# Two decode layers on one core: output weights of two key heads loaded as four adjacent rows a partition

## The chip, the cores and the metric

The kernel runs on one core of a Trainium2 chip. The metric is the device time of one execution in microseconds, as the median of several runs; lower is better. A profile is one more execution, recorded by the hardware profiler; times within it count from the first instruction of that execution.

## What is computed

Two identical layers for four sequences with one new token each. A layer is attention over a cached context, with 32 query heads in 8 key heads (4 query heads share a key head), followed by a feed-forward block. Both layers use the same caches and weights, all in bfloat16.

```python
def _A_ref(x, k_cache, v_cache, wq, wo):
    q = (x @ wq)  # as [4, 32, 1, 128]
    ...
    scores = jnp.einsum("bhqd,bhkd->bhqk", q, k) * (Dh ** -0.5)
    p = _softmax(scores, axis=-1)
    o = jnp.einsum("bhqk,bhkd->bhqd", p, v)
    return (lambda x, *d: x.transpose(*d))(o, 0, 2, 1, 3).reshape(B, Sq, Hq * Dh) @ wo

def _B_ref(x, w_gate, w_up, w_down):
    return (_gelu(x @ w_gate) * (x @ w_up)) @ w_down

x = A_x
x = x + _A_ref(_layernorm(x, axis=-1), A_k_cache, A_v_cache, A_wq, A_wo)
x = x + _B_ref(_layernorm(x, axis=-1), B_w_gate, B_w_up, B_w_down)
...
```

The last two lines are done a second time. Shapes: x is 4 x 512, each cache 4 sequences x 8 key heads x 4096 positions x 128, `wq` 512 x 4096, `wo` 4096 x 512, the feed-forward weights 512 x 1792 and 1792 x 512. One sequence's keys or values of one key head are 1 MB, so the caches are 64 MB in all.

## The kernel before, in words

**Order of the work.** `attend_first` does sequence 0 of layer 1. Then a loop runs over the sequences b = 0 to 3: the feed-forward block of layer 1 for b (`dense_first` for 0, `dense` for the others), and then a stage that mixes layer 2 of sequence b with layer 1 of sequence b + 1 (`attend(b + 1)`). Where the prediction speaks of sequence 1, 2 or 3, it means layer 1 of that sequence, the second half of `attend(1)`, `attend(2)` and `attend(3)`. After the last block come `attend_last`, layer 2 of sequence 3 (the last stage), and `dense_last`, the feed-forward of layer 2 for all four sequences at once. Layer 2 reuses a few value tiles that layer 1 left in place; most of the cache is read twice.

**Tiles and buffers.** A cache tile is half of one key head's context, 128 partitions with 16 positions of 128 numbers, 4 KB a partition and 512 KB in all. Eight value tiles have slots (`VRing`, L682), keys have sixteen. Every load is issued on SyncE's queue (SP), in program order. A value load is issued as soon as the step that last used its slot has ended, so the ring of slots paces the loads. All instructions of an engine run in the order that the program gives.

**Value steps.** `Values.step` (L828) multiplies one value tile with the softmax's probabilities. For a streamed head the result is in rows (`stream_v`, L786, matmuls of L791); DVE turns it (`turn_v`, L799) and sums and scales it (`sum_v`, L801, with L806 and L807) into `OT_bf` or, in layer 2, `OT2_bf`: attention outputs with the 128 numbers of a head on the partitions and the heads along the free axis. Unstreamed heads use L859 and are scaled by L680; the last head of a sequence is one of them. Scaling is done when a head, or a pair of heads, has both its tiles; `hold=True` puts it off until `flush`. Results lie in PSUM, in two banks in turn; in `attend` the streamed heads of the second group use the banks `ps_sc`, `ps_sm` and `ps_sc`, and the last head `ps_sm` again.

**Output weights.** `wo_sb` holds, for each of the 32 query heads, 128 rows of 512, row d on partition d: 1 KB a partition and head. `load_rest` (L158) loads it in four pieces of eight heads, at the end of `attend_first`, with the feed-forward weights behind it on the queue. `RowProj.heads` (L401) multiplies a head's output with its weights into 512-wide rows (matmul of L405, four heads in four column groups at a time); `split` (L409) brings the row sums to bfloat16 in two parts, with a ScalarE copy (L412) and a DVE operation (L413); `onto` adds them to the column-wise result `y`. `OutProj.heads` (L385, matmuls of `mac`, L275) does the remaining heads directly into `y`. So the final order of a sequence is: row sums of most heads, split, the last pair of heads directly, the split added, the rest of that pair.

**Fillers.** `busy(n, ...)` (L479, matmuls of L482) issues n matmuls whose result nobody reads.

**Head order.** The two groups of four key heads swap from sequence to sequence. Sequences 0 and 2 take heads 0 to 3 first, sequences 1 and 3 take heads 4 to 7 first. In `attend`, `heads` lists the pairs of key heads in the order of their value steps: row sums of `heads[0]`, `heads[1]` and `heads[2]` are placed between value steps (L1230 to L1240), `heads[3]` goes through `OutProj`. In `attend_last` (L1252) the pair of key heads 2 and 3 comes first, then 0 and 1, then 4 and 5; head 7 is the last.

**The last stage's tables.** ScalarE needs a function table for gelu; L1291 loads it ahead of the value steps of the last group.

Of the kernel before, what the change touches and what calls it, by code (L numbers as in the profile page):

```python
# [30 lines left out]
WD_PARTS = (0, 6, 10, 12, 13, 14)  # L31
ROWS_A = 8
UP_ROWS = 8


@with_exitstack
def kernel(
# [111 lines left out]
    def cache_tile(cache, b, kvh, t):  # L149
        if whole(b, kvh):  # L150
            return cache[b, kvh].rearrange("(p t c) d -> t p c d", t=NT, p=P)[t]
        return cache[b, kvh].rearrange("(t p c) d -> t p c d", t=NT, p=P)[t]

    def load_wq(g):
        n = HG * Dh
        dq.dma_start(out=wq_sb[g][:], in_=wq_dram[:, :, g * n:(g + 1) * n])

    def load_rest():  # L158
        n = Hq // 4
        for i in range(4):  # L160
            dq.dma_start(out=wo_sb[:, i * n:(i + 1) * n], in_=wo_dram[:, i * n:(i + 1) * n])  # L161
        dq.dma_start(out=wg_sb[:], in_=B_w_gate.rearrange("(k p) n -> p k n", p=P))
        dq.dma_start(out=wu_sb[:], in_=B_w_up.rearrange("(k p) n -> p k n", p=P))
        wd_dram = B_w_down.rearrange("(k p e) n -> p k e n", p=P, e=2)
        wd_pairs = wd_sb.rearrange("p (k e) n -> p k e n", e=2)
        for lo, hi in zip(WD_PARTS, WD_PARTS[1:]):
            if hi - lo > 1:
                own = slice(lo // 2, hi // 2)
                dq.dma_start(out=wd_pairs[:, own], in_=wd_dram[:, own])
            else:  # L170
                dq.dma_start(out=wd_sb[:, lo], in_=wd_dram[:, lo // 2, lo % 2])
# [201 lines left out]
    def nothing(t):  # L373
        nc.scalar.copy(out=t, in_=qb[:, 0:1].broadcast_to([P, t.shape[1]]))
# [207 lines left out]
    def scores(sc, g, t, runs=together):  # L582
        for run in runs:
            scores_of(sc, g, [(s, t) for s in run])
# [224 lines left out]

    class Values:  # L810
        def __init__(self, layer, b, tiles, prob, dst, keeps=(), streamed=(), paired=(), sums=None, park=(),
                     last_bank=None, off_ot=False, last_width=WEIGHT):
            self.streamed, self.sums, self.park = streamed, sums or {}, park
            self.paired, self.last_bank, self.off_ot = paired, last_bank, off_ot
            self.last_width = last_width
            self.layer, self.b, self.tiles, self.n = layer, b, list(tiles), 0
            self.prob, self.dst, self.keeps = prob, dst, keeps
            self.seen, self.ot, self.late = {}, None, []
# [65 lines left out]
        def unit(self, kvh):  # L884
            pair = [2 * (kvh // 2), 2 * (kvh // 2) + 1]
            alone = kvh in self.streamed and kvh not in self.paired
            return [kvh] if self.tiles[-1][0] in pair or alone else pair

        def scale(self, ot, unit, rden):
            n, s = len(unit), unit[0] % GH  # L890
            if unit[0] in self.streamed:
                turn_v(ot, n)
                return sum_v(ot, self.dst(unit[0], n), rden[:, s:s + n], n)
            scaled(self.dst(unit[0], n), ot[:, s % 2:s % 2 + n, :rep], rden[:, s:s + n])
# [64 lines left out]
    def attend_first():  # L959
# [5 lines left out]
        last = one(b)[-1][0]  # L965
        vals = Values(1, b, one(b), prob1, dst1(b), keeps=kept,
                      streamed=[h for h in range(Hkv) if h != last],
                      paired=[h for h in range(Hkv) if h // 2 != last // 2])
        ring.extend(1, b, one(b))
        load_wq(gx)  # L970
        keys.load_heads(GH)
# [40 lines left out]
        vals.step(3)  # L1012
        scores(sc1, gy, 1, last_alone)
        vals.step(3, hold=True)
        p0 = soft(sc1)
        vals.flush()
        soft_turn(p0)
# [117 lines left out]
    def attend(b, qy, before, norm, early=None):  # L1135
# [11 lines left out]
        vals1 = Values(1, b, one(b), prob1, dst1(b), keeps=kept1,  # L1147
                       streamed=[gy * GH + s for s in range(GH - 1)], park=apart1,
                       sums={4: (ps_sc, "sc"), 5: (ps_sm, "sm"), 6: (ps_sc, "sc")},
                       last_bank=lambda: ps_sm.tile([P, 2, WEIGHT], FP32, name="ot", tag="sm"))  # L1150

        sc2 = [new_scores(early=True)]
        if early:
# [59 lines left out]
        turn(4)  # L1213
        vals1.step(3)
        scores(sc1, gy, 1, last_alone)
        p0 = soft(sc1)
        vals1.step(3)
        x = swap_tile()
# [11 lines left out]
        vals1.step(2)  # L1230
        rows.heads(heads[0], hp)
        vals1.step(2)
        rows.heads(heads[1], hp)
        vals1.step(1)
        proj = OutProj(o1(b), 1)
        spare = proj.bank[:, KD * WEIGHT:]
        rows.heads(heads[2], rep)
        busy(3, spare)
        vals1.step(1)
        rows.heads(heads[2] + rep, rep)  # L1240
        rows.split()
        busy(5, spare)
        vals1.step(1)
        proj.heads(heads[3], rep)
        vals1.step(1)
        assert vals1.left() == 0
# [5 lines left out]
    def attend_last(q_bf, norm, before, late):  # L1252
        b = B - 1
        gx, gy = second_groups[b]
        prob2 = {}
        kept2, own2, other2, apart2 = two(b)
        tiles = kept2 + own2 + apart2 + other2
        vals = Values(2, b, tiles, prob2, dst2(b),
                      streamed=[h for h in range(Hkv) if h != tiles[-1][0]],
                      paired=[h for h in range(Hkv) if h // 2 != tiles[-1][0] // 2],  # L1260
                      last_width=WIDE)
        sc2 = [new_scores(early=True)]
        scores(sc2[0], gx, 0)
        ring.pump_tile(late[0], k_tile(gx * GH + 2, 0))
        ring.pump_halves(late[1], k_tile(gx * GH + 3, 0))
        scores(sc2[0], gx, 1)
        q_spread_apart(q_sums(q_bf[:]))
        p0 = soft(sc2[0], norm)
        for _ in range(2):
            before.fill()  # L1270
        before.turn()
        sc2.append(new_scores(early=True))
        scores(sc2[1], gy, 0)
        scores(sc2[1], gy, 1)
        soft_turn(p0)
        before.sum()
        pe0, den0 = soft_swap(p0), soft_den(p0)
        p1 = soft(sc2[1], norm, lasting=True)
        prob2[gx] = (pe0, soft_recip(den0))
        rows = RowProj(o2)  # L1280
        vals.step(8, hold=True)
        soft_turn(p1)
        vals.flush()
        pe1, den1 = soft_swap(p1), soft_den(p1)
        prob2[gy] = (pe1, soft_recip(den1))
        heads = pairs(tiles)
        homes = [(ps_x, "x", ROWS_A), (ps_h, "h", KF - ROWS_A)]
        full = [pool.tile([P, n * WIDE], FP32, name="gr", tag=tag) for pool, tag, n in homes]
        for part in full:
            nothing(part[:])  # L1290
        nc.scalar.preload_act_table_set("gelu_apprx_tanh_and_others")  # L1291
        vals.step(4)
        rows.heads(heads[0], hp)
        rows.heads(heads[1], hp)
        vals.step(2)
        rows.heads(heads[2], hp)
        rows.split()
        vals.step()
        proj = OutProj(o2, B, WIDE)
        proj.heads(heads[3], rep)  # L1300
        vals.step()
        rows.onto(proj)
        proj.n = Hq - rep
        proj.heads(heads[3] + rep, rep)
        part = banks.tile([P, UP_ROWS * WIDE], "ur")
        nothing(part[:])
        spare = ps_sc.tile([P, 512], FP32, name="spare", tag="sc")
        busy(1, spare[:])
        squares = wq_sb[1][:, 3].bitcast(FP32)[:, :B * (KD + 1)].rearrange("p (b k) -> p b k", b=B)
        nc.vector.memset(squares[:, :, KD], D * LN_EPS / P)  # L1310
        assert vals.left() == 0 and ring.at == len(ring.seq)
        return proj.y, full + [part], squares
# [260 lines left out]
```

## Time and profile before

| | |
|---|---|
| median of 3 runs | 268.15 us (266.75 to 268.27) |
| profiled execution, its own time | 268.99 us |
| its span, first to last instruction | 267.2 us |
| mean granted TensorE clock | 0.866 |
| TensorE matmul busy | 195.1 us (73%) |
| VectorE busy | 182.2 us (68%) |
| ScalarE busy | 66.0 us (25%) |
| moved by DMA | 103.05 MB, mean 386 GB/s |
| four loads of `wo_sb` | 1024 KB each, 12.0 us from issue to landing |

How to read it: the page cuts the span into 40 equal slices (6.68 us each) and gives, per engine, the busy share in tenths, the granted clock of TensorE (PEclk) and what the DMA engines moved. A row of the timeline has start, duration, engine, line of the kernel, operation, output and inputs, shape, count and, in brackets, how long the engine had been idle before it and what ended that wait; several equal instructions in a row are merged, so a duration of "x16" spans all sixteen. A matmul's end includes its drain, and the next may start before it. The chain that ended last is followed backwards from the last instruction: each piece was released by the one above it.

### The profile page before, as it was taken

The page shows a single profiled execution, that of the slowest core. Times are in us where ns is not written, and L with a number is a line of the kernel's source. Part 1 is how long each engine was busy: PE and PEld are TensorE (multiplying, and loading weights), DVE is VectorE, ACT ScalarE, POOL GpSimd, SP SyncE. Part 2 cuts the span into 40 slices and gives each one's busy share as a digit, 9 for nine tenths or more (in the row PEclk, how much of TensorE's full clock was granted, in tenths as well). Part 3 has the DMA queues.
Part 4 walks back from the last instruction along what each step waited for, and adds up shares of the span by engine and source line. Part 5 has one row for each costly group of instructions (what it writes and reads, how often), then busy time and mean ns, then how long its engine had stood idle before and what let it go on. Part 6 is the DMA issues. An engine that isn't in the chain of part 4 may idle for free.

```text
span 267.2 us, 8596 instructions
## 1 busy us (share of the span) xinstructions
PE 195.1 (73%) x3767; PEld 114.8 (43%) x3775; DVE 182.2 (68%) x448; ACT 66.0 (25%) x136; POOL 3.9 (1%) x10
## 2 busy tenths in 40 slices
PE   1396246544689796989678968787788687888884
PEld 1333123322255453557436245464363354553563
DVE  3385955451335899884776998746769996568773
ACT  1001001100222422032323520304136103044642
POOL 2000000000001000000000000000000000000001
PEclk9998555655597959799999985899999979999999
DMA  7999999999994999999999999999999999999940
GB/s 244 432 416 421 423 429 417 408 385 406 413 412 177 394 416 417 420 417 400 390 414 416 416 419 421 416 415 375 403 418 418 421 415 418 420 405 405 413 160 3
DMA packets 30732, 103.05 MB, mean 386 GB/s; under 512 B 2788, under 2 KB 7144, under 8 KB 29672
## 3 DMA queue, kind: packets, MB, share of 16 engines
q1 hardware_dynamic: 30672, 102.51, 95.7%
q8 instruction: 29, 0.48, 0.6%
q14 instruction: 7, 0.06, 0.1%
q10 hardware_dynamic: 24, 0.01, 0.0%
HBM read 102.50 MB, written 0.00 MB: 384 GB/s over the span
## 4 chain that ended last, share of the span: by engine, by line
DMA 51%; PE 21%; DVE 16%; SPq 6%; ACT 3%; issue 3%; DVEq 0%
DMA v_t<-in_A_v_cache_dram 25%; DMA kp<-in_A_k_cache_dram 8%; DMA kw<-in_A_k_cache_dram 8%; PE sc L592 6%; DMA wu_sb<-in_B_w_up_dram 5%; DMA kw<-in_A_v_cache_dram 4%; SPq L161 4%; DVE kp L537 3%; PE ot L859 3%; DVE kw L537 3%; PE y L275 3%; PE so L791 2%; PE q L309 1%; DVE q L315 1%; DVE qb L360 1%
## 5 line engine op out<-in xcount | busy, mean ns | idle before, releaser
L592 PE MATMUL sc<-kw,qb 128*32 128x512 bf16 x244 | 39.6, 446 | 5.2 <-DVE kw L537 2.2
L592 PE MATMUL sc<-kp,qb 128*32 128x512 bf16 x268 | 40.1, 450 | 1.0 <-DVE kp L537 0.2
L592 PEld LDWEIGHTS <-qb 128*32 128x32 bf16 x512 | 23.1, 104 | 39.6 <-issue 21.4
L537 DVE STREAM_TRANSPOSE kw<-kw 128x1024 f32<-128x1024 f32 x32 | 38.0, 1215 | 0.7 <-DMA kw<-in_A_k_cache_dram 0.6
L537 DVE STREAM_TRANSPOSE kp<-kp 128x1024 f32<-128x1024 f32 x32 | 36.7, 1199 | 0.0
L859 PE MATMUL ot<-pe,v_t 128*128 128x32 bf16 (+1 forms) x896 | 30.0, 184 | 5.6 <-DMA v_t<-in_A_v_cache_dram 2.8
L859 PEld LDWEIGHTS <-v_t 128*128 128x128 bf16 x896 | 27.7, 100 | 13.7 <-issue 7.4
L614 ACT ACTIVATE pe<-sc,nl 128x512 bf16<-128x512 f32 x8 | 5.5, 687 | 85.9 <-DVE pe L611 67.6
L791 PE MATMUL so<-v_t,pe 128*32 128x256 bf16 x304 | 15.0, 319 | 13.6 <-DMA v_t<-in_A_v_cache_dram 11.6
L799 DVE STREAM_TRANSPOSE so<-so 128x512 f32<-128x512 f32 (+1 forms) x23 | 13.8, 599 | 11.1 <-PE so L791 11.1
L791 PEld LDWEIGHTS <-pe 128*32 128x32 bf16 x320 | 9.1, 105 | 19.4 <-issue 12.5
L602 DVE TENSOR_REDUCE pe<-sc 128x1 f32<-128x512 f32 x12 | 8.3, 691 | 9.2 <-PE sc L592 9.1
L405 PE MATMUL yr<-wo_sb,OT_bf 128*2 128x512 bf16 (+1 forms) x120 | 10.7, 425 | 4.9 <-DMA wo_sb<-in_A_wo_dram 4.9
L647 PE MATMUL x<-pe,ident_bf 128*32 128x128 bf16 x192 | 5.4, 233 | 11.8 <-DVE pe L622 11.8
L647 PEld LDWEIGHTS <-ident_bf 128*32 128x32 bf16 x256 | 5.3, 100 | 16.1 <-issue 14.1
L791 PE MATMUL so<-v_t,pl 128*32 128x256 bf16 x192 | 9.4, 275 | 3.3 <-DMA v_t<-in_A_v_cache_dram 3.3
L650 ACT CAST pe<-x 128x512 bf16<-128x512 f32 x12 | 7.0, 586 | 17.4 <-PE x L647 17.4
L275 PE MATMUL q<-xb,wq_sb 128*128 128x5 bf16 (+1 forms) x192 | 5.7, 173 | 6.5 <-DMA wq_sb<-in_A_wq_dram 6.5
L353 PE MATMUL qe<-q_bf,ident_bf 128*32 128x16 bf16 (+1 forms) x272 | 5.7, 176 | 5.6 <-DVE q_bf L335 2.9
L622 DVE STREAM_TRANSPOSE pe<-pe 128x512 bf16<-128x512 bf16 x12 | 8.4, 696 | 1.1 <-ACT pe L614 1.1
L275 PEld LDWEIGHTS <-wo_sb 128*128 128x128 bf16 x160 | 7.6, 101 | 3.3 <-DMA wo_sb<-in_A_wo_dram 2.6
L482 PEld LDWEIGHTS <-ident_bf 128*128 128x128 bf16 x63 | 5.2, 99 | 8.7 <-issue 4.3
(172 smaller groups left out, 255.2 us busy)
## 6 DMA issues: line engine op xcount, KB each, us to landing
v_t<-in_A_v_cache_dram SPq DMA_DIRECT2D x89, 512.0 KB, 8.5
kp<-in_A_k_cache_dram SPq DMA_DIRECT2D x32, 512.0 KB, 9.9
kw<-in_A_k_cache_dram SPq DMA_DIRECT2D x24, 512.0 KB, 9.6
wq_sb<-in_A_wq_dram SPq DMA_DIRECT2D x2, 2048.0 KB, 7.7
kw<-in_A_k_cache_dram SPq DMA_DIRECT2D x4, 1024.0 KB, 11.6
v_t<-in_A_v_cache_dram SPq DMA_DIRECT2D x4, 1024.0 KB, 14.2
wo_sb<-in_A_wo_dram SPq DMA_DIRECT2D x4, 1024.0 KB, 12.0
wq_sb<-in_A_v_cache_dram SPq DMA_DIRECT2D x3, 1024.0 KB, 11.8
```

Source lines behind the costliest of these rows:

```text
L161: dq.dma_start(out=wo_sb[:, i * n:(i + 1) * n], in_=wo_dram[:, i * n:(i + 1) * n])
L275: nc.tensor.matmul(dst, lhsT=lhsT, rhs=rhs, start=first, stop=last, skip_group_check=True)
L405: nc.tensor.matmul(self.rows[j:j + x.shape[1]], lhsT=x, rhs=wo_sb[:, i], start=self.n < QD, stop=True, skip_group_check=True)
L537: nc.vector.transpose(out=words, in_=words)
L592: nc.tensor.matmul(sc[s * QS:(s + 1) * QS], lhsT=qb[:, w0:w0 + 2 * W], rhs=kt[:, :, be // 2, :, be % 2], start=(t == 0 and be == 0), stop= ...
L602: nc.vector.tensor_reduce(out=m, in_=sc.rearrange("p c j -> p (c j)"), axis=AX.X, op=ALU.min if norm else ALU.max)
L622: nc.vector.transpose(out=flat, in_=flat)
L647: nc.tensor.matmul(x[a * QS:(a + 1) * QS, s], lhsT=ident_bf[:, s * QS:(s + 1) * QS], rhs=pT[:, a], start=True, stop=True, skip_group_check ...
L650: nc.scalar.copy(out=pe, in_=x.rearrange("p s t c h -> p (s t c h)"))
L791: nc.tensor.matmul(ps[d, :NW * QS], lhsT=x[:, w:w + NW].rearrange("p c h -> p (c h)"), rhs=v[:, i:i + NW, d], start=first and i == 0, stop ...
L799: nc.vector.transpose(out=flat, in_=flat)
L859: nc.tensor.matmul(self.ot[:, s % 2], lhsT=v[:, i, :], rhs=wide(pe[:, s, t * CH + i, :], self.ot.shape[-1]), start=(done == 0 and i == 0), ...
```

## The change

Key heads 0 and 1 (query heads 0 to 7, listed by the new constant `QUADS = (0,)`, the pair number) get another layout of their output weights. Within the 512 rows of one key head's four query heads, partition p now holds rows 4p to 4p + 3, which are adjacent in memory: 4 KB in one piece instead of four pieces of 1 KB. Position j of the four then holds row 4p + j, which belongs to query head p // 32 and to its number 4 (p mod 32) + j. The other three pairs are loaded as before.

The attention outputs of these eight heads are brought into the same order before they meet the weights. `Values.regroup` does this: for each j and each of the four heads, a matmul with every fourth column of the identity picks 32 numbers of the head and puts them on the 32 partitions of that head's group, in a PSUM bank that the heads used before; one ScalarE copy puts the result back in place of the old outputs.

Where it is called, and what moves:

- Sequence 0: between the value steps of heads 2 and 3 and the softmax of the second group.
- Sequence 2: after the scores of the second group, ahead of the softmax and three value steps.
- Sequences 1 and 3, where heads 0 to 2 come late: after the second value step of head 2, whose scaling is put behind it. Only half of `heads[1]`'s rows stand where all of them stood, the other half takes the place of the first half of `heads[2]`; all eight rows of `heads[2]` come after the first value step of the last head, with the split behind them. Three fillers instead of five.
- Last stage: `rows.heads(heads[0])` ahead of the four value steps instead of behind them, those steps with their scaling held, then regroup for all four sequences at once, then the scaling; the table load behind all that.

```diff
+QUADS = (0,)
...
     def load_rest():
         n = Hq // 4
-        for i in range(4):
-            dq.dma_start(out=wo_sb[:, i * n:(i + 1) * n], in_=wo_dram[:, i * n:(i + 1) * n])
+        wo_quads = A_wo.rearrange("(i p j) n -> p i j n", p=P, j=QD)
+        to_quads = wo_sb.rearrange("p (i j) n -> p i j n", j=QD)
+        for kvh in range(0, Hkv, 2):
+            if by_quads(kvh):
+                dq.dma_start(out=to_quads[:, kvh:kvh + 2], in_=wo_quads[:, kvh:kvh + 2])
+            else:
+                i = kvh * rep
+                dq.dma_start(out=wo_sb[:, i:i + n], in_=wo_dram[:, i:i + n])
...
+        def regroup(self):
+            kvh, n = self.due[0][1][0], sum(len(unit) for _, unit in self.due)
+            assert n == 2
+            ps = self.due[-1][0]
+            self.due = []
+            if len(ps.shape) == 3:
+                ps = ps.rearrange("p a b -> p (a b)")
+            o = self.quads[:, kvh * rep:(kvh + n) * rep].rearrange("p (v h) b -> p v h b", h=rep)
+            nb = o.shape[3]
+            turned = ps[:, :n * QD * nb].rearrange("p (v j b) -> p v j b", j=QD, b=nb)
+            for j in range(QD):
+                for h in range(rep):
+                    nc.tensor.matmul(turned[h * QS:(h + 1) * QS, :, j], lhsT=ident_bf[:, j::QD],
+                                     rhs=o[:, :, h], start=True, stop=True, skip_group_check=True)
+            nc.scalar.copy(out=o, in_=turned)
...
         def scale(self, ot, unit, rden):
             n, s = len(unit), unit[0] % GH
+            if self.quads is not None and by_quads(unit[0]):
+                self.due.append((ot, unit))
...
         vals.step(3, hold=True)
+        vals.regroup()
         p0 = soft(sc1)
...
         scores(sc1, gy, 1, last_alone)
+        if by_quads(gx * GH):
+            vals1.regroup()
         p0 = soft(sc1)
...
-        rows.heads(heads[1], hp)
+        late_unit = by_quads(gy * GH)
+        if late_unit:
+            middle, end = (heads[1] + rep, rep), (heads[2], hp)
+            rows.heads(heads[1], rep)
+        else:
+            middle, end = (heads[2], rep), (heads[2] + rep, rep)
+            rows.heads(heads[1], hp)
         vals1.step(1)
         proj = OutProj(o1(b), 1)
         spare = proj.bank[:, KD * WEIGHT:]
-        rows.heads(heads[2], rep)
+        rows.heads(*middle)
         busy(3, spare)
-        vals1.step(1)
-        rows.heads(heads[2] + rep, rep)
+        vals1.step(1, hold=late_unit)
+        if late_unit:
+            vals1.regroup()
+            vals1.flush()
+            busy(3, spare)
+            vals1.step(1)
+        rows.heads(*end)
         rows.split()
-        busy(5, spare)
-        vals1.step(1)
+        if not late_unit:
+            busy(5, spare)
+            vals1.step(1)
         proj.heads(heads[3], rep)
...
+        rows.heads(heads[0], hp)
+        vals.step(4, hold=True)
+        vals.regroup()
+        vals.flush()
         nc.scalar.preload_act_table_set("gelu_apprx_tanh_and_others")
-        vals.step(4)
-        rows.heads(heads[0], hp)
         rows.heads(heads[1], hp)
```

`by_quads(kvh)` is `kvh // 2 in QUADS`. The three `Values` objects get the output tile as `quads`; `due` collects the units of these heads that have been scaled.

## Prediction, written before the result was known

> **What bounds the kernel now.** I read the page first (busy rows, the 40 slices, packet counts), then the windows around the weight load, then the chain that ended last, then the timeline of the stages that the change edits. Of the page:
>
> ```profile
> span 267.2 us, 8596 instructions
> ...
> PEclk9998555655597959799999985899999979999999
> DMA  7999999999994999999999999999999999999940
> GB/s 244 432 416 421 423 429 417 408 385 406 413 412 177 394 416 417 420 417 400 390 414 416 416 419 421 416 415 375 403 418 418 421 415 418 420 405 405 413 160 3
> DMA packets 30732, 103.05 MB, mean 386 GB/s; under 512 B 2788, under 2 KB 7144, under 8 KB 29672
> ```
>
> The DMA row is 9 in 36 of 40 slices: the 16 DMA engines bound nearly all of the kernel. It falls short at the start, in slice 13 (177 GB/s, 80 to 87 us) and in the tail. So two things are worth time: less transfer ahead of a stage that waits for its last byte, and less work between the last bytes and the end. Slice 9 (385 GB/s, 53 to 60 us) is the output weights. Two windows, whose last columns are DMA share and GB/s:
>
> ```profile
> 48.00:50.00 2.00, 1.63 (x34) 1.08 (x34) 0.26 (x1) 1.02 (x2) 0.00 (x0) 0.75 1.03 416
> 58.00:60.00 2.00, 0.32 (x8) 0.10 (x7) 1.02 (x4) 0.00 (x0) 0.00 (x0) 0.50 1.09 386
> ```
>
> Cache tiles (4 KB a row) move at 416, output weights (1 KB a row) at 386, both with the engines full: the short rows cost rate. PE starts on these landings (timeline, PE alone):
>
> ```profile
> 57.06 1.02 PE L405 MATMUL yr<-wo_sb,OT_bf 128*2 128x512 bf16 x8 [1.62 <-DMA wo_sb<-in_A_wo_dram]
> 59.76 1.02 PE L405 MATMUL yr<-wo_sb,OT_bf 128*2 128x512 bf16 x8 [1.68 <-DMA wo_sb<-in_A_wo_dram]
> ...
> 73.94 0.93 PE L1323 MATMUL u<-wu_sb,xb 128*8 128x448 bf16 x16 [0.40 <-DMA wu_sb<-in_B_w_up_dram]
> ```
>
> PE waits for each megabyte of output weights, 2.70 us apart, and at 73.94 for the up weights. Whatever the load saves moves 73.94, the block that follows it and the end of the thin slice 13.
>
> **1, the load (load_rest).** The first of four 1 MB loads changes from 1024 rows of 1 KB to 256 rows of 4 KB. At the tiles' rate a megabyte takes 2.70 x 386 / 416 = 2.51 us: 0.19 saved, and everything behind it lands 0.19 earlier. Bounds: 0 (no rate gained) to 0.27 (slice 6 runs at 429). I take 0.19, from rows of the new length one stage earlier. SP issues fewer descriptors, so the loads queued behind go out earlier, but they land in the same order on engines that are full. By the Trainium skill's page DMA: Bandwidth & Descriptors, Specifications, rows from 512 B on run at line rate: 1 KB rows would lose nothing and the whole change would end at + 0.49. Its section Why small descriptors are slow gives a fixed cost of about 3 cycles a packet: my estimate by it (35 beats for 32 against 131 for 128) is a gain of 0.17. The two windows agree with the second and not with the first.
>
> **2, the reordering (regroup).** Sixteen matmuls with 32 weight columns, then one ScalarE copy of 8 columns (32 in the last stage). The nearest rows for a price, and two waits that cover it:
>
> ```profile
> 130.83 0.40 PE L791 MATMUL so<-v_t,pl 128*32 128x256 bf16 x8 [0.59 <-DMA v_t<-in_A_v_cache_dram]
> ...
> 133.25 0.27 PE L353 MATMUL qe<-q_bf,ident_bf 128*32 128x16 bf16 x16 [0.63 <-DVE q_bf L335]
> ...
> 169.86 0.69 DVE L554 TENSOR_SCALAR park<-v_t 128x512 int32<-128x512 int32 x1 [0.50 <-DMA v_t<-in_A_v_cache_dram]
> ...
> 257.43 0.38 ACT L374 CAST ur<-qb 128x256 f32<-128x256 bf16 x1
> ```
>
> PE: 0.27, from sixteen matmuls of the same weight shape (bounds 0.2 and 0.6). The copy: below the 0.38 of a 256-column cast; I take 0.25 and 0.1 of hand-over, together 0.35 (bounds 0.15 and 0.48).
> Sequence 0: regroup stands between value steps and a softmax; the copy puts up to 0.35 ahead of the softmax's exponential on ACT. What follows it is over before 57.06, where PE waits 1.62 for weights: hidden. Sequence 2: it stands ahead of three value steps and delays DVE's scale by 0.27 at most, ahead of a DVE copy that waits 0.50 for its tile: hidden. Without these waits each would cost about 0.3.
>
> **3, sequences 1 and 3 of layer 1.** Four rows of weights move back, eight come after the next value step, busy(5) becomes busy(3). Chain that ended last, in sequence 3, and the split's two rows in the timeline:
>
> ```profile
> 231.21 0.40 PE so L791 x8
> 231.61 0.22 PE yr L405 x4
> 231.83 0.65 PE y L482 x5
> 232.48 0.61 PE ot L859 x16
> 233.09 0.92 PE y L275 x16
> 234.01 0.48 PE ot L859 x16
> 234.50 0.23 PE y L275 x4
> 234.76 0.65 PE y L275 x16
> ```
>
> ```profile
> 231.93 0.59 ACT L412 CAST yt<-yr 128x512 bf16<-128x512 f32 x1 [4.74 <-PE yr L405]
> ...
> 232.55 0.75 DVE L413 SCALAR_TENSOR_TENSOR yt<-yt,masks,yr 128x512 bf16<-128x512 bf16 x1
> ```
>
> Now the row sums end at 231.83; their split (0.59 on ACT, 0.75 on DVE) is ready at 233.30, well before PE takes it up at 234.50. After: tiles land 0.19 earlier, so the first value step ends at 231.42; regroup 0.27 and three fillers (3/5 of 0.65) bring PE to 232.08, which covers the copy, for whose PSUM bank the next value step waits. That step still waits for its tile and ends at 233.09 - 0.19 = 232.90. Eight rows, twice 0.22, end at 233.34. The split: + 0.10 hand-over + 0.59 + 0.03 + 0.75 = 234.81. PE has done its 0.92 and 0.48 by 234.74 and waits until about 234.86; the four split matmuls (0.23) and the last rows (0.65), which also need the last head's scale, queued on DVE behind the split, end at 235.75 against 235.41 before. That is + 0.34: + 0.53 from the edit, - 0.19 from the landing. Bounds for the edit: + 0.2 (split hidden, regroup alone) to + 0.8. The next norm is queued behind these rows, and from 235 to 254 work follows work, so it carries.
> Sequence 1 gets the same + 0.34, but at 130.83 PE waits 0.59 for a tile that lands 0.19 earlier: 0.40 of cover, absorbed. If that cover goes, it is + 0.34 more.
>
> **4, the last stage.** The rows of heads[0] go ahead of four value steps, then regroup, then the scaling; the ACT table load moves behind regroup's copy. DVE and ACT, then PE alone, then the chain's end:
>
> ```profile
> 253.58 0.18 DVE L807 TENSOR_TENSOR OT_bf<-ov,rden 128x8 bf16<-128x8 f32 x1
> ...
> 254.45 1.28 ACT L1291 ACT_TABLE_LOAD   x1
> ```
>
> ```profile
> 253.83 1.06 PE L791 MATMUL so<-wq_sb,pl 128*32 128x256 bf16 x32 [0.36 <-ACT pl L650]
> 254.71 1.04 PE L405 MATMUL yr<-wo_sb,OT_bf 128*4 128x512 bf16 x16
> 255.84 0.62 PE L791 MATMUL so<-wq_sb,pl 128*32 128x256 bf16 x16
> 256.29 0.60 PE L405 MATMUL yr<-wo_sb,OT_bf 128*4 128x512 bf16 x8
> ```
>
> ```profile
> 246.32 11.96 DMA kw<-in_A_v_cache_dram
> 258.32 0.38 PE ot L859 x8
> 258.95 0.56 PE y L275 x16
> ```
>
> Before, the last tile's landing ends the chain: PE takes its second half at 258.32, and the last rows start at 258.95. After, with the + 0.34: the outputs of heads[0] stand at 253.58 + 0.18 + 0.34 = 254.10; eight rows take 0.44 (1.04 - 0.60), to 254.59; four value steps 0.88 (254.71 - 253.83), to 255.47; regroup to 255.74; its copy to 256.07, with PE idle; eight rows to 256.51; two value steps 0.45 (256.29 - 255.84), to 256.96; the last eight rows, 0.60 with their drain, to 257.56. Split: + 0.05 + 0.59 + 0.03 + 0.75 = 258.98. The table load, 256.07 + 1.28 = 257.35, ends 0.25 ahead of the split; it is what is late next. The last head's scale waits on DVE for the split, and the last rows start at 259.25: + 0.30. The last tile, now at about 258.1, no longer ends the chain; the split does.
>
> **Sum.** The span of the profiled execution goes from 267.2 to 267.5, its own time from 268.99 to 269.3. It is 0.84 above the median of the runs, 268.15; on the median 268.45, said as 268.4. One per cent is 2.7 us, about what a measurement of this kernel can tell from no change.
>
> **The rivals.**
> Hidden: the moves fit beside the waits after all, the last landing still ends the chain and the load alone counts: 268.15 - 0.19 = 268.0. For it: each addition is under 0.6 and stands near a wait. Against: the split of sequence 3 has 1.2 of slack (233.30 to 234.50) and I move its start by 1.5.
> Queue: sequence 1's + 0.34 is not absorbed, since later value steps also free their slots later: 268.8, or 269.0 if sequence 3 loses as much again in part. For it: GB/s in slices 19, 20 and 28 is 400, 390 and 375, so the queue runs thin there; against: the DMA digit stays 9.
> No gain from the load: the low rate at 58 has another cause than the row length; 268.15 + 0.49 = 268.6. This is also what the first of the two rules above would give. Against: the rate falls with these loads and rises behind them.
> Slower by over 1%: the granted clock. PEclk is 9 in the six last slices but 5 in slices 5 to 7, where PE waits for data. Eight rows of L405 take 1.02 at 57.06 and 0.60 at 256.29, the same work at half and at full clock. If two fillers fewer and a few idle stretches of 0.3 bring one half-speed slice (6.7 us) into 231 to 264, and PE is half of the path there, it costs 6.7 x 0.5 x (1.02 / 0.60 - 1) = 2.3: 270.7. It decides from a little more than one slice on. Against: PE already idles that long in those slices, and they stay at 9. By the Trainium skill, TensorE: Matmul & The Clock Gate, What's actually happening, the clock follows activity in free-running windows of about 3.4 us. No run here shows how their phase falls in the changed kernel.
>
> **How the numbers follow.** Forecast (0 to 0.7 slower) 0.48; hidden 0.24; queue 0.13; no gain 0.05; clock 0.07; a faster clock in slices 13 to 17 and 24 to 26, where it is now 5 to 8 for three slices in all, 0.03. The likeliest gives 268.4. Low end: hidden, with the spread of the runs (lowest 266.75): 266.5. High end: queue at 269.0 with a part of the clock's price: 270.2. Faster by over 1%: 0.03, the faster clock. Slower: 0.08, the clock and a little of the queue. Within 1%: 0.89.
>
> **What the profile of the changed kernel would show.** Step 1: packets under 2 KB down from 7144 to about 6120, packets in all down by 768, the first L405 group near 56.9 and the up weights near 73.75. Step 2: sixteen PE matmuls of about 0.27, with no wait on the copy in sequences 0 and 2. Step 3: the split ending 1.5 after the row sums, and PE waiting a tenth for it in sequences 1 and 3; in sequence 1 still a wait for a tile near 130.6. Step 4: an idle stretch of 0.3 on PE behind regroup, and the split, not the last tile, as the releaser of the last rows. I am wrong if 73.94 does not move, if DMA idles near 130, if the last tile still ends the chain, or if the clock's digits change after 231.

## The result, and the profile after

| | before | after |
|---|---|---|
| median of 6 runs each, same chip | 268.21 us | 271.67 us |
| ratio after / before | | 1.0126, 95% interval 1.0081 to 1.0172 |
| profiled execution, its own time | 268.99 | 272.34 |
| its span | 267.2 | 270.6 |

The change makes the kernel slower by about 1%. Ratios here and below are taken from the runs in the faster of the chip's two states, so they can differ a little from those of the medians. Measured again later beside other kernels, the same code gave 270.05 against 268.52, ratio 1.0071 (1.0034 to 1.0108). Both intervals hold 1.0081 to 1.0108, a loss of 2.2 to 2.9 us. The prediction, 268.4 with a range from 266.5 to 270.2, was wrong: it had the change as good as free.

The page of the changed kernel, the rows that the prediction showed of before:

```profile
span 270.6 us, 8759 instructions
...
PEclk9998556555688868899999998999999979999999
DMA  7999999999995999999999999999999999999930
GB/s 248 432 418 418 425 428 414 419 386 409 412 369 198 371 415 418 415 421 409 347 406 420 417 417 420 417 417 393 402 422 416 417 423 414 417 324 384 419 117 3
DMA packets 29966, 103.07 MB, mean 381 GB/s; under 512 B 2788, under 2 KB 6120, under 8 KB 28904
```

Packets under 2 KB fell from 7144 to 6120, packets in all by 766. The clock's digits after 231 are still 9. The DMA digits look as before, but the row of rates beneath does not: slice 20 (128 to 135 us) is 347 where it was 390, slices 36 and 37 (237 to 250 us) are 324 and 384 where they were 405 and 405. Of these two places the second is the telling one: slice 20 is also 355 to 366 in experiments 1, 3, 5 and 11 below, which lose 0.4 us at most by their best estimates. TensorE alone around the output weights, as in the prediction:

```profile
56.85 1.02 PE L415 MATMUL yr<-wo_sb,OT_bf 128*2 128x512 bf16 x8 [1.44 <-DMA wo_sb<-in_A_wo_dram]
...
73.78 0.93 PE L1371 MATMUL u<-wu_sb,xb 128*8 128x448 bf16 x16 [0.60 <-DMA wu_sb<-in_B_w_up_dram]
```

The first row was at 57.06 and the second at 73.94: the load's gain of about 0.2 is there. The chain that ended last, in sequence 3 and at the end (start, duration):

```profile
223.86 9.89 DMA v_t<-in_A_v_cache_dram
233.76 0.05 issue
233.80 0.65 PE ot L870 x16
234.46 0.53 PE yr L415 x8
234.99 1.03 PE y L285 x16
236.02 0.48 PE ot L870 x16
236.52 0.90 PE y L285 x20
237.42 0.33 PE so L801 x8
...
248.23 13.40 DMA kw<-in_A_v_cache_dram
261.63 0.05 issue
261.67 0.38 PE ot L870 x8
```

From the value step on the last head's first tile to the next step of layer 2 (`so`) it is now 233.80 to 237.42, 3.62; before it was 232.48 to 235.41, 2.93. And the last tile (`kw`) still ends the chain: it lands at 261.63 instead of 258.28, 3.35 later, which is the whole growth of the span (3.4).

So the time went into the loads. One stretch of them, 12 us from 2 us after the first load that SP issues behind sequence 3's chain, before and after (last columns: DMA share, GB/s):

```profile
237.79:249.79 12.00, 9.68 (x253) 4.98 (x245) 10.11 (x33) 6.30 (x14) 0.00 (x0) 1.00 1.02 401
```

```profile
239.79:251.79 12.00, 9.41 (x253) 4.86 (x245) 10.11 (x33) 6.31 (x14) 0.00 (x0) 1.00 0.96 360
```

Ten per cent of the rate over 12 us is 1.2 us. The part of the list of issues that holds that first load gives its time from issue to landing (the last number). Before, it was issued at 235.79:

```profile
v_t<-in_A_v_cache_dram SPq DMA_DIRECT2D x1, 512.0 KB, 5.5
```

After, at 237.79:

```profile
v_t<-in_A_v_cache_dram SPq DMA_DIRECT2D x1, 512.0 KB, 4.5
```

The load needs a slot that the layer-2 step behind the chain frees, and SP issues nothing ahead of it: no load for 5.27 us before (230.52 to 235.79) and for 6.56 after (231.23 to 237.79). Meanwhile the engines work off what was queued. I call the time from that issue to its landing the lead: how much the queue still held. It shrank by 1.0.

### The profile page after: what moved, and what is told of

Same layout as the page of the kernel before. It is cut to its first block, busy times and chain, and to the rows that moved or that the text cites. A ratio compares the mean times of both kernels' runs of the same rounds, so it can differ in the third digit from the quotient of the medians.

```text
span 270.6 us, 8759 instructions
## 1 busy us (share of the span) xinstructions
PE 194.0 (72%) x3843; PEld 115.4 (43%) x3851; DVE 182.4 (67%) x448; ACT 66.7 (25%) x141; POOL 3.9 (1%) x10
## 2 busy tenths in 40 slices
DMA packets 29966, 103.07 MB, mean 381 GB/s; under 512 B 2788, under 2 KB 6120, under 8 KB 28904
## 4 chain that ended last, share of the span: by engine, by line
DMA 45%; DVE 20%; PE 20%; SPq 9%; issue 2%; ACT 2%; DVEq 0%; ACTq 0%
DMA v_t<-in_A_v_cache_dram 29%; DMA kp<-in_A_k_cache_dram 8%; DVE kp L547 7%; PE sc L602 6%; DVE kw L547 6%; DMA kw<-in_A_v_cache_dram 5%; PE ot L870 4%; DMA wd_sb<-in_B_w_down_dram 4%; SPq L171 3%; PE y L285 2%; SPq L179 2%; PE so L801 2%; PE q L319 1%; DVE pe L612 1%; DVE q L325 1%
## 5 line engine op out<-in xcount | busy, mean ns | idle before, releaser
L602 PE MATMUL sc<-kw,qb 128*32 128x512 bf16 x244 | 39.0, 448 | 4.8 <-DVE kw L547 1.9
L602 PE MATMUL sc<-kp,qb 128*32 128x512 bf16 x268 | 38.8, 436 | 1.1 <-DVE kp L547 0.2
L564 DVE TENSOR_SCALAR park<-v_t 128x512 int32<-128x512 int32 x12 | 7.8, 676 | 1.5 <-DMA v_t<-in_A_v_cache_dram 1.4
```

The lines of the kernel that those rows point to most:

```text
L564: nc.vector.tensor_scalar(out=t[:], in0=words[:, self.at:self.at + n], scalar1=0, scalar2=None, op0=ALU.bitwise_or)
L602: nc.tensor.matmul(sc[s * QS:(s + 1) * QS], lhsT=qb[:, w0:w0 + 2 * W], rhs=kt[:, :, be // 2, :, be % 2], start=(t == 0 and be == 0), stop= ...
```

## The experiments

Theories. **Chain**: the change lengthens the work between the last head's tile and the next norm in sequences 1 and 3, which delays SP's next loads, and the loss is more than the delay. **Cover** (the prediction): sequence 1's delay disappears in a wait for a tile, sequence 3's counts one for one. **Work**: the added instructions cost wherever they stand. All kernels were timed in five rounds beside the kernel before. In microseconds (0.01 of the ratio is 2.7):

| kernel | ratio to before (95%) | us |
|---|---|---|
| load alone | 0.9991 (0.9968 to 1.0015) | -0.2 |
| order of sequences 1 and 3 alone | 1.0068 (1.0031 to 1.0105) | +1.8 |
| order of the last stage alone | 1.0016 (1.0000 to 1.0032) | +0.4 |
| regroup alone | 1.0059 (1.0034 to 1.0085) | +1.6 |
| whole change, 1 and 3 mended | 1.0008 (0.9975 to 1.0041) | +0.2 |
| before, chain rearranged | 1.0045 (1.0007 to 1.0083) | +1.2 |
| before, 5 fillers in 1, 2 and 3 | 1.0073 (1.0040 to 1.0107) | +2.0 |
| before, 10 fillers in 1 | 1.0036 (1.0011 to 1.0060) | +1.0 |
| the change again | 1.0071 (1.0034 to 1.0108) | +1.9 |
| mended, then 5 fillers in 1 and 3 | 1.0104 (1.0079 to 1.0130) | +2.8 |
| before, chain trimmed | 1.0016 (0.9992 to 1.0040) | +0.4 |
| before, 10 fillers in 3 | 1.0084 (1.0057 to 1.0112) | +2.3 |
| the change, 1 mended | 1.0052 (1.0026 to 1.0078) | +1.4 |
| the change, 3 mended | 1.0043 (1.0018 to 1.0068) | +1.2 |

**1. The load alone**: the new load, no regroup, the order of before. It leaves the reordering out, so query heads 0 to 7 meet their rows of weights in another order.

```diff
-        vals.regroup()
...
-            vals1.regroup()
```

> Only the load of key heads 0 and 1 is changed; nothing is reordered, so the attention outputs of these eight heads meet the weights in another order and the result differs. Queue theory (the late order in sequences 1 and 3 starves the DMA queue): this part is worth the 0.2 us that the weights land earlier, so 0 to 0.4 us faster than before, and the DMA's loss between 80 and 90 us, 0.9 in the profile after, is chance. Load theory (the new landing times themselves spoil the first thin stage, 80 to 90 us): at least 0.5 us slower, with 34 MB reached about 0.7 later than in the profile before.

-0.2 (-0.9 to +0.4). The load is not what costs; a gain of 0.19 can be neither seen nor excluded.

**2. The order of sequences 1 and 3 alone**, on the kernel before, without regroup.

```diff
+        late_unit = gy == 0
...
+        vals1.step(1, hold=late_unit)
+        if late_unit:
+            vals1.flush()
+            busy(3, spare)
+            vals1.step(1)
```

> The order of sequences 1 and 3 of layer 1 as in the change (eight rows and the split behind the last head's first value step, three fillers for five), with the old load and no regroup. Queue theory: most of the loss is here, 1.5 to 2.5 us slower than before; the chain to the next norm is 0.4 to 0.6 longer in both sequences, the value load that follows it is issued later by more than that in sequence 3, and DMA falls below 9 tenths near 240 us. Load theory and regroup theory: within 0.5 us of before.

+1.8 (0.8 to 2.8), five times the 0.34 of the prediction. Its chain behind the last head's first tile is 0.64 longer, as in the changed kernel.

**3. The last stage's order alone.**

```diff
-        nc.scalar.preload_act_table_set("gelu_apprx_tanh_and_others")
-        vals.step(4)
         rows.heads(heads[0], hp)
+        vals.step(4, hold=True)
+        vals.flush()
+        nc.scalar.preload_act_table_set("gelu_apprx_tanh_and_others")
```

> The order of the last stage alone as in the change (rows of heads 8 to 15 ahead of four value steps, their scaling held, the table load behind), with the old load and no regroup. Queue theory: within 0.4 us of before, since the last tile's landing still ends the chain. If the last stage were the cause: at least 1 us slower, with the split or the table load ending last instead of the landing.

+0.4 (0.0 to 0.9). What the prediction forecast for this order alone is worked out under part 4 below.

**4. Regroup alone**: in all five places, with the old load and the order of before, so that outputs are reordered whose weights are not.

```diff
+LOADS = ()
...
+        vals1.step(1, hold=gy == 0)
+        if gy == 0:
+            vals1.regroup()
+            vals1.flush()
         rows.heads(heads[2] + rep, rep)
```

> The sixteen matmuls and the copy of regroup in all five places, with the old load and the order of before (in sequences 1 and 3 right behind the second value step of head 2, ahead of the last four rows); the outputs of these eight heads are reordered and the weights are not, so the result differs. Queue theory: the chain in sequences 1 and 3 grows by the 0.3 of the matmuls and the wait for the copy, 0.3 to 0.6 each, so 0.5 to 1.5 us slower than before. Load theory: within 0.5 us of before. Regroup theory (the extra instructions and the wait for their copy are the cost, the order is not): 2 us slower or more.

+1.6 (0.9 to 2.3). In its trace the step on the last head's first tile starts 0.68 and 0.51 after that tile's landing in sequences 1 and 3 (0.04 and 0.05 before): here the delay stands ahead of the step, behind the landing. Chain and Work are not told apart by this one.

**5. The whole change, mended**: everything is kept, but in sequences 1 and 3 regroup comes one step earlier, and rows, split and fillers stand ahead of the last head's tile again.

```diff
+            vals1.regroup()
+            busy(3, spare)
+            vals1.step(1)
+            rows.heads(heads[2], hp)
...
         rows.split()
         busy(5, spare)
         vals1.step(1)
```

> The whole change, but in sequences 1 and 3 regroup comes right after head 2's first value step, and the eight reordered rows, the split and the five fillers stand ahead of the last head's first value step, as before. All the work of the change is kept; only what lies behind the last tile of the sequence is as it was. Chain theory (what counts is the time from the last value tile to the norm, since no load is issued in that stretch): the stretch without an issue is back near 5.0 and 5.3 us, and the time at 268.2 to 269.0 (the last stage's order may keep 0.4). Work theory (regroup costs wherever it stands): 269.8 to 270.5, what regroup alone cost. Cover theory (the prediction on record): 268.1 to 268.4.

+0.2 (-0.7 to +1.1): the loss is gone with all of the change's work still there. Work falls. TensorE in sequence 3 of this kernel:

```profile
229.13 0.28 PE L912 MATMUL so<-OT_bf,ident_bf 128*32 128x2 bf16 x16
...
230.35 0.62 PE L415 MATMUL yr<-wo_sb,OT_bf 128*2 128x512 bf16 x8
230.90 0.72 PE L492 MATMUL y<-wg_sb,ident_bf 128*128 128x256 bf16 x5
231.46 0.64 PE L870 MATMUL ot<-pe,v_t 128*128 128x64 bf16 x16
...
233.77 0.65 PE L285 MATMUL y<-OL_bf,wo_sb 128*128 128x64 bf16 x16
```

In sequence 3, regroup and eight rows fit ahead of the tile: the step starts 0.13 after the tile's landing (231.46 for 231.33). From step to last matmuls it is 2.31 again, 2.32 before (232.44 to 234.76), 2.96 in the changed kernel (233.80 to 236.76).

In sequence 1 they do not fit: the tile lands at 120.56 and the step starts at 121.19, 0.63 later. Counted from the landing, that chain is as long (2.95) as in the changed kernel (3.01; before 2.37). Experiment 4 had such a late step in both sequences and cost 1.6. So this kernel mends sequence 3, and in sequence 1 it only moves the delay from behind the step to ahead of it; the loss is gone all the same.

**6. The chain of before, rearranged to be shorter.**

```diff
-        rows.split()
         busy(5, spare)
         vals1.step(1)
-        proj.heads(heads[3], rep)
+        rows.heads(heads[3], rep)
         vals1.step(1)
+        rows.split()
+        proj.heads(heads[3] + rep, rep - 1)
         rows.onto(proj)
-        proj.n = Hq - rep
-        proj.heads(heads[3] + rep, rep)
+        proj.n = Hq - 1
+        proj.heads(heads[3] + hp - 1, 1)
```

> The kernel before, with its chain behind the last tile made shorter: head 2's four output heads go as four row matmuls (0.22 us) in place of sixteen column matmuls (0.92), the split comes after the last value step, and the last head's matmuls surround the split's. Same sums, other order. Chain theory: the chain from the last tile's value step to the norm goes from 2.97 to about 2.45, the stretch without an issue from 5.0 and 5.3 to about 4.5 and 4.8, and the time falls by 1.0 to 2.0 us, to 266.2 to 267.2. Cover theory and any account in which the full DMA queue decides: within 0.3 of 268.2.

+1.2 (0.2 to 2.2): the expectation was wrong. Sequence 3:

```profile
234.44 0.65 PE L859 MATMUL ot<-pe,v_t 128*128 128x64 bf16 x16
235.03 0.39 PE L405 MATMUL yr<-wo_sb,OT_bf 128*2 128x512 bf16 x4
235.69 0.66 PE L859 MATMUL ot<-pe,v_t 128*128 128x64 bf16 x16 [0.28 <-DMA v_t<-in_A_v_cache_dram]
236.61 0.53 PE L275 MATMUL y<-OL_bf,wo_sb 128*128 128x64 bf16 x12 [0.26 <-DVE OL_bf L680]
237.27 0.40 PE L275 MATMUL y<-masks,yt 128*128 128x64 bf16 x4
237.51 0.28 PE L275 MATMUL y<-OL_bf,wo_sb 128*128 128x64 bf16 x4
```

I had overlooked that the last head's second step waits for a tile of its own, 1.25 after the first. The matmuls I removed had filled that wait; the split, now later, came behind it. From the first step to the last matmuls it is 3.07 instead of 2.32, so a kernel that I meant to shorten is a third case of a longer chain, and slower. (Experiments 6, 7 and 11 edit code that sequence 2 shares, so they act there too, which the first two expectations leave out.)

**7. Five fillers** between head 2's matmuls and the last value step of before.

```diff
         proj.heads(heads[3], rep)
+        busy(5, spare)
         vals1.step(1)
```

> The kernel before with five more fillers (0.65 us) between head 2's output matmuls and the last value step, in sequences 1 and 3, and nothing else: no new load, no regroup, no other order. The delay is that of the change, 0.64. Chain theory: each sequence loses 0.65 to 1.2, the time is 269.5 to 270.6, about what the order of these two sequences alone cost (270.3). Cover theory: sequence 1's part is absorbed by the wait of 0.59 near 131, so 268.8 to 268.9. Work theory (the change's own instructions are the cost): fillers are harmless, 268.2 to 268.5.

+2.0 (1.1 to 2.9). Idle work of 0.55 a sequence, in three sequences (1.65), costs about as much as the change. That is against Work. Cover would come to 0.55 in sequence 3 and at most as much in sequence 2, 1.1 in all, the low end of the interval; since sequence 2 had its part, this run gives no price for one place.

**8 and 12. Ten fillers in one sequence**, 1 or 3.

```diff
+        busy(10 if b == 1 else 0, spare)
```

> The kernel before with ten more fillers (1.3 us) at the same place in sequence 1 alone. Chain theory: the tile that is waited for near 131 is issued only behind the delayed norm, so it comes later too and the wait is still there; 269.5 to 270.4. Cover theory: 1.3 less the 0.59 of that wait, 268.9, and the wait near 131 is gone.

> The kernel before with ten more fillers ahead of the last value step in sequence 3 alone (1.1 to 1.3 us, the same dose as was given to sequence 1 alone, which cost 1.0). Chain theory: 1.0 to 2.0 above before, the more the nearer this place is to the end. Cover theory: as the prediction on record had it, one for one, 1.1 to 1.3.

+1.0 (0.3 to 1.6) in sequence 1, +2.3 (1.5 to 3.0) in sequence 3, each for a delay of 1.09. In 1 the time does not tell Chain from Cover, and neither does the trace: of the wait near 131, which one expected to stay and the other to go, 0.28 is left at 130.68 (0.59 before), and new waits of 0.51 and 0.75 follow at 132.64 and 134.11. In 3 the time excludes one for one. Sequence 3, the fillers, then the lead and the rate behind it:

```profile
233.26 1.25 PE L482 MATMUL y<-wg_sb,ident_bf 128*128 128x256 bf16 x10
234.35 0.65 PE L859 MATMUL ot<-pe,v_t 128*128 128x64 bf16 x16
```

```profile
v_t<-in_A_v_cache_dram SPq DMA_DIRECT2D x1, 512.0 KB, 4.5
```

```profile
238.29:250.29 12.00, 9.48 (x253) 4.87 (x246) 10.11 (x33) 6.29 (x14) 0.00 (x0) 1.00 0.96 366
```

A kernel without any of the change shows its picture: lead 4.5, share 0.96, 366 GB/s.

**9 and 10. The change again, and the mended kernel with the change's delay.**

```diff
         proj.heads(heads[3], rep)
+        busy(5 if b != 2 else 0, spare)
         vals1.step(1)
```

> The changed kernel once more, beside the three that follow. Its chain behind the tile is 0.64 us longer in sequences 1 and 3 than before. If a microsecond of that chain costs about one of the time, as one sequence alone showed, it is 269.8 to 270.3 where before is 268.5; if the two delays and the reordering elsewhere add up as the first four runs did, 271.5 to 272.5.

> The whole change with regroup early, and rows, split and fillers ahead of the tile as before (which cost nothing), and five more fillers ahead of the last value step in sequences 1 and 3 alone: the change's work with the change's delay (0.54 to 0.65), but not its order. Chain theory: the same time as the changed kernel beside it, within 0.8. Order theory (something in the moved rows or the late split costs beyond the delay): half of the changed kernel's loss or less.

+1.9 (0.9 to 2.9) and +2.8 (2.1 to 3.5), 0.9 apart and within each other's intervals. Five fillers take the mended kernel from +0.2 to at least the change's loss; the delay makes it, not the order.

**11. The chain of before, trimmed**: four matmuls moved into TensorE's wait for the last scale.

```diff
-        proj.heads(heads[3], rep)
+        proj.heads(heads[3], rep - 1)
         vals1.step(1)
...
         rows.onto(proj)
+        proj.heads(heads[3] + rep - 1, 1)
```

> The kernel before with four of head 2's sixteen output matmuls moved from ahead of the last value step to behind the split's, where TensorE now waits about 0.2 us for the last head's scale; in sequences 1, 2 and 3, which share this code. Chain theory: each chain ends 0.15 to 0.2 earlier and the time is 0.2 to 0.8 below before. Any other account: no change.

+0.4 (-0.2 to +1.1), no gain. The chain did get shorter, from 2.32 to 2.18 (232.16 to 234.34), but the lead and the rate are those of before:

```profile
v_t<-in_A_v_cache_dram SPq DMA_DIRECT2D x1, 512.0 KB, 5.5
```

```profile
237.37:249.37 12.00, 9.64 (x253) 4.86 (x245) 10.11 (x33) 6.30 (x14) 0.00 (x0) 1.00 1.00 398
```

So 0.14 taken out of the chain gave nothing that can be measured; two for one, in sequences 1 and 3, would have gained 0.6, outside the interval.

**13 and 14. The change with one sequence mended**: `if b == 1:` (or 3) takes the order of experiment 5, else that of the change.

> The changed kernel with sequence 1 mended (regroup early; rows, split and fillers ahead of the tile as before) and sequence 3 as the change has it. Lead theory (the first load behind the delayed norm is issued with less work left in the queue, 4.5 to 4.7 us ahead of its landing where it was 5.47, and the next four megabytes then lose 1.1 to 1.7): sequence 3 alone loses that, and the time is 1.1 to 2.0 above before. Prediction on record: sequence 3 costs 0.34, 268.9 where before is 268.5.

> The changed kernel with sequence 3 mended and sequence 1 as the change has it. Lead theory: sequence 1's first load behind the norm has a lead of 4.7 to 4.9 in place of 5.45 and the time is 0.4 to 1.0 above before (1.08 of fillers there cost 1.0). Prediction on record: the delay is absorbed by the wait near 131, no change.

With sequence 3 alone as in the change +1.4 (0.7 to 2.1), with sequence 1 alone +1.2 (0.5 to 1.8). Cover's 0.34 and 0 are outside these intervals. The sum, 2.6, lies in the change's 2.2 to 2.9, but it holds twice what both share with experiment 5 (load, sequences 0 and 2, last stage and what is left in the mended sequences: +0.2, -0.7 to +1.1), so the split between the two sequences is not sharp. In the profile of 14 the lead of sequence 1's load is 5.4, not the 4.7 to 4.9 that was expected.

**Lead and rate in sequence 3.** One profile each (that of experiment 2, whose execution took 3.6 us more than that kernel's median, is left out; it has 4.7 and 366); lead to the tenth, mean rate in the 12 us chosen as above:

| lead, us | kernels (by experiment) | GB/s |
|---|---|---|
| 5.5 | before, 11 | 401, 398 |
| 5.2 to 5.4 | 1, 3, 5, 7, 8, 14 | 391, 401, 386, 388, 388, 382 |
| 5.0 | 4, 6 | 372, 369 |
| 4.7 | 9, 13 | 370, 376 |
| 4.5 | after, 12 | 360, 366 |
| 3.9 | 10 | 360 |

From 5.2 up the mean is 392, from 5.0 down 368: 6% of 12 us, 0.7. Single profiles differ too: the four kernels whose code in sequence 3 is that of before (before, 1, 3, 8) read from 388 to 401. In sequence 1 the lead does not sort the kernels (385 on average from 5.3 up, 380 below): the mended orders of 5 and 13 have 4.8 and 4.9 there, the changed order of 14 has 5.4. So the lead is an account of sequence 3 only. In 10, TensorE also ran at half its clock from 226 to 231, ahead of this stretch, which made its lead shorter still.

## Why the prediction was wrong, point by point

**Part 1, the load: right.** 73.94 became 73.78, 0.16 earlier for 0.19. All the profiles show it: from the landing of the last tile ahead of it to its own, the megabyte takes 2.50 on average with the new load (seven kernels, 2.46 to 2.55) and 2.67 with the old (nine, 2.61 to 2.76), 0.17 less. The Trainium skill's DMA: Bandwidth & Descriptors, Why small descriptors are slow, led to 0.17; the trace agrees, and its Specifications' line rate from 512 B on does not fit. But 0.2 us is below what the timing can tell (experiment 1).

**Part 2, regroup: right.** Sequence 3 of the changed kernel:

```profile
232.22 0.28 PE L912 MATMUL so<-OT_bf,ident_bf 128*32 128x2 bf16 x16
...
232.61 0.17 ACT L914 CAST OT_bf<-so 128x8 bf16<-128x8 f32 x1 [4.53 <-PE so L912]
...
233.80 0.65 PE L870 MATMUL ot<-pe,v_t 128*128 128x64 bf16 x16 [0.87 <-DMA v_t<-in_A_v_cache_dram]
```

0.28 for 0.27; 0.17 of copy and 0.11 of hand-over for 0.25 and 0.1. The covers of sequences 0 and 2 held as far as the time can tell: experiment 5 keeps all five regroups, these two as in the change, and costs nothing that can be measured.

**Part 3, sequences 1 and 3: the step that failed.** The chain itself was nearly right. Its edit is +0.64 for +0.53. In the second profile of the changed kernel (experiment 9) the tile is used at 232.17, 0.27 earlier than before, and the `so` step that ends the chain comes 0.37 later, 235.71 for 235.34; the prediction had +0.34. That the two come so close is partly luck: the edit was 0.11 more, and the 0.27 is not the load's alone, since the issue-free stretch near 80 us is 0.7 shorter in that profile than before (last section). Wrong was what follows, in two places.

The first: "from 235 to 254 work follows work, so it carries". I carried the delay one for one along the engines. It goes into the loads: SP's first issue moves from 235.79 to 236.16, the same 0.37, the lead from 5.5 to 4.7, and in that profile megabytes 94 to 98 take 0.8 longer than before, in the first one 1.5 (counted from the packets). In time, sequence 3 cost 1.4 for a chain 0.64 longer (experiment 13), and a delay of 1.09 cost 2.3 (experiment 12): about 2 for 1.

The second: "0.40 of cover, absorbed", in sequence 1. The tile waited for at 130.83 was itself issued behind the delayed chain: at 125.34 before, at 126.59 after (0.62 of these 1.25 were there ahead of the chain, at the first tile's step). Layer-2 steps of sequence 1's stage in the changed kernel:

```profile
131.10 0.67 PE L801 MATMUL so<-v_t,pl 128*32 128x256 bf16 x16
133.61 0.40 PE L801 MATMUL so<-v_t,pl 128*32 128x256 bf16 x8 [0.57 <-DMA v_t<-in_A_v_cache_dram]
134.85 0.40 PE L801 MATMUL so<-v_t,pl 128*32 128x256 bf16 x8 [0.58 <-DMA v_t<-in_A_v_cache_dram]
```

The prediction still had a short wait near 130.6; it is gone, but there are two at 133.61 and 134.85, where before had none (132.21 and 133.45). The second profile of the same code has none of the three, so where the time goes varies. What speaks against absorption is the time of experiment 14: +1.2 (0.5 to 1.8) for 0, though the rest of the change is in it too. The reason is argued from the order of issue and not shown by a run: a wait for a load is no cover for work that the load's issue waits for.

**Part 4, the last stage.** "The last tile, now at about 258.1, no longer ends the chain; the split does" is wrong for the changed kernel, because the loads came 3.35 later: the split was done at 261.13, the tile landed at 261.63. Where the loads are not late, it is right: in the profile of experiment 3 the tile landed at 257.89, and the last rows waited for the split, done at 258.58. The +0.30 held sequence 3's +0.34; without it the same sum puts the split at 258.64 and the last rows at 258.91, level with 258.95 before. So for the order alone it forecast nothing, and the measured +0.4 (0.0 to 0.9) reaches down to that.

**The rivals.** Queue named the mechanism ("later value steps also free their slots later", and that the queue runs thin in slices 19, 20 and 28), and I gave it 0.13 and 0.34 to 0.6 us; the loss was 2.2 to 2.9. What I held against it, that the DMA digit stays 9, was no evidence: the digit stays 9 in the changed kernel while slice 36 falls to 324 GB/s. The clock rival falls: the digits after 231 stay at 9.

**What stays open.** Why a queue that still holds 4.5 us of transfers loses rate. In the changed kernel's slow stretch the engines' share falls from 1.02 to 0.96, but the rate falls by 10%, so packets there also take longer; no run separates the two. Nor is sequence 1 explained. By experiment 14 it loses up to 1.2, for a delay behind the step; by experiment 5, with as long a delay ahead of the step, nothing that can be measured; the intervals overlap, and neither lead nor rate tells the two apart. Nor is it shown why the mended sequence 3 of experiments 5 and 14, with a lead of 5.3, has a rate of 386 and 382, below the 401 of before. A part of the profiled 3.4 belongs to that execution: between 80 and 89 us it lost 0.9 against the load's gain, which the second profile of the same code did not.

## What to carry to other kernels

When loads are paced by freed buffers, follow a delay to the next load's issue and not only to the next instruction: read how long the queue is at that issue (issue to landing) and take a delay there for possibly more than itself, about double in sequence 3 here. Before a wait for a tile is counted as cover, look whether that tile's issue depends on the added work. Put additions ahead of the last tile that a chain waits for, as far as they fit before it lands; with that order the whole change cost nothing measurable (experiment 5), while regroup where it made that step 0.5 to 0.7 late in both sequences cost 1.6 (experiment 4).

## What the runs showed of the hardware beyond that

The stretch behind the feed-forward weights has two lengths, whatever the kernel: SP issues no load from about 74 on for 9.1 us in five of these profiles (before, after, 2, 13, 14) and for 8.1 to 8.5 in the other eleven, among them experiment 9, the same code as after. What differs is TensorE's clock: from 80 to 83 us the granted clock is 0.50 to 0.55 in the five and 1.00 in the eleven. Two rows of before and of experiment 3, whose program is the same up to there:

```profile
81.59 0.63 PE L592 MATMUL sc<-kp,qb 128*32 128x512 bf16 x2
```

```profile
81.86 0.40 PE L592 MATMUL sc<-kp,qb 128*32 128x512 bf16 x2
```

The same two matmuls take 0.63 and 0.40. The Trainium skill's TensorE: Matmul & The Clock Gate, What's actually happening, puts the clock down to activity in free-running windows; that the same code meets either clock agrees with this. A difference of 0.8 us between two single profiles therefore says nothing here until the clock of that stretch is compared.
